# Two single expert slots replaced by one shared slot of 96 and 32 rows in column groups

## The chip, the core and the metric

The kernel runs on one core of a Trainium2 chip. The metric is the device time of one execution in microseconds; before the change it is 801.86, the median of three runs (801.76 to 804.71).

## What is computed

Three stages follow each other on a tensor of 4 batches x 576 tokens x 512 channels: attention with a threshold on the scores, a mixture of experts, and a mixing stage over tokens and channels. The change is in the second:

```python
for b in range(B):
    prev_e = -1
    for s in range(S):
        fresh_e = int(np.argmax(logits[b, s]))
        e = fresh_e if s == 0 or local_gate[b, s] < 0.5 or prev_e < 0 else prev_e
        prev_e = e
        p = np.exp(logits[b, s] - logits[b, s].max()); p /= p.sum() + 1e-09
        h = np.maximum(x[b, s] @ w1[e], 0.0)        # 512 -> 1024
        out[b, s] = p[e] * (h @ w2[e])              # 1024 -> 512
```

There are 8 experts. Each has 2 MB of w1 and 2 MB of w2 in float32. How many tokens each gets depends on the data, so the kernel counts them and reads which expert a piece of work belongs to from a table that it has filled itself.

## The kernel before, in words

**Slots.** Tokens are listed by expert in DRAM. An expert's list is cut into tiles of 128 rows. A *slot* is a piece of work with a fixed place in the program; its expert and its first row come from the table. A paired slot does two tiles of one expert (256 tokens), a single slot does one. Three early slots run while the last batch is still being routed (a single, a pair, a single). Then come eight paired late slots, and then two single ones (`NFINAL = 2`). What doesn't fit runs in extra single slots behind a branch (`self.total > 0`). Which experts get the two single slots is decided in `late_slots` (L691 to L744) by a key: experts with an odd number of tiles left come first, and the two largest keys win. `slot_table` (L746) turns the counts into rows and expert numbers.

**A paired or single slot.** TensorE multiplies in fp32r, with each operand split in a high and a low part, and three products: high x high, high x low, low x high (L1241 to L1243, L1256 to L1258 for pairs; L1272 to L1274, L1317 to L1319 for singles). ScalarE makes the high part and VectorE the low one (L1352, L1355), of w1 into the two tiles `stk`, of w2 into a ring of three. In a single slot the last quarter of w1 and of w2 isn't split; it is multiplied in full fp32 (L1280, L1321). A single slot has tokens as rows of the result, so its hidden values are turned by transposes (L1300) before the second product.

**Order.** TensorE, ScalarE and VectorE run in the order in which the code is written (`manual_schedule`); waits between engines are added by the framework. SP issues all weight loads in its own order: a load waits there until the buffer that it overwrites has been read. The steps of a slot are software-pipelined: `slot_step` handles the slot in hand (`now`), loads and splits the next (`nxt`) and finishes the last (`last`, `old`). A load of w1 or w2 is conditional (`cond`): it is skipped where the expert is that of the slot before.

**Work put in between.** The weights of the third stage come as 64-bit floats and are decoded by VectorE, ScalarE and GpSimd in small steps (`decode`, L1476), some of which stand between a slot's instructions. `more_words` (L1399) has SP stage two pieces of the channel weights, into a ring of two. `load_first_x` (L1619) loads the first batch for the third stage into `raw`, whose space w1 uses till then.

**Behind the last slot.** ScalarE scales the output by the gate (L1335), GpSimd scatters the rows to DRAM (L1342), all engines pass the branch for extra slots (L814), and TensorE begins the third stage with transposes (L1635).

Of the kernel before, what the change touches and what calls it, by code (L numbers as in the profile page):

```python
# [21 lines left out]
DM = H * D  # L22
E, F = 8, 1024
G = E + 1
P = 128
# [6 lines left out]
NEARLY, NTWOS, NFINAL, MAXSINGLE = 2, 8, 2, 8  # L32
# [4 lines left out]
RING, HIDDEN_STEPS, LAST_STEPS = 3, 8, 10  # L37
# [16 lines left out]
class Kernel:  # L54
# [10 lines left out]
    def constants(self):  # L65
# [23 lines left out]
        nc.vector.memset(self.first[0:1, 0:1], -1e30)  # L89
        n = MAXSINGLE  # L90
# [4 lines left out]
        for k, w in ((0, 1), (1, 2), (2, 1), (3, P), (4, 2 * P), (5, P)):  # L95
            nc.gpsimd.iota(i[:, k], pattern=[[w, n]], base=0, channel_multiplier=0)
        self.slotk = self.small("slotk", [1, 2, 3 * n])
        nc.gpsimd.tensor_copy(self.slotk, i[:, :6].rearrange("p (t k) n -> p t (k n)", t=2))
        self.starts = self.small("starts", [1, 3, E + 1])
        nc.gpsimd.memset(self.starts, 1.0)  # L100
        nc.gpsimd.memset(self.starts[:, :, 0:1], 0.0)
        self.late_counts, self.early_counts = (self.small(f"{n}_counts", [1, k, E + 1]) for n, k in (("late", 3), ("early", 2)))
        for t in (self.late_counts, self.early_counts):
            nc.gpsimd.memset(t, 0.0)
        b = scr[0:1, 160:160 + 3 * (E + 1)].rearrange("p (k e) -> p k e", k=3)
        nc.gpsimd.iota(b, pattern=[[0, 3], [NT // P, E + 1]], base=0, channel_multiplier=0)
        self.bases = self.small("bases", [1, 3, E + 1])
# [583 lines left out]
    def late_slots(self):  # L691
# [23 lines left out]
        one, two, fin = (counts[:, k, 1:] for k in range(3))  # L715
        nc.vector.scalar_tensor_tensor(fin, key, top[:, NFINAL - 1:NFINAL], has, ALU.is_ge, ALU.mult)
# [5 lines left out]
        nc.vector.tensor_tensor(bases[:, 2, :E], bases[:, 1, :E], nf, ALU.add)  # L722
# [19 lines left out]
        nc.vector.tensor_tensor(tabi[:, 2, n + 1:], e[:, n + 1:], e[:, n:3 * n - 1], ALU.not_equal)  # L742
# [41 lines left out]
    def first_loads(self):  # L784

        self.w1raw = [self.w1r] + [self.raw[:, i * F:(i + 1) * F] for i in range(3)]
        slots = [("early", 0, False), ("early", NEARLY, True), ("early", 1, False)]
        slots += [("late", MAXSINGLE + j, True) for j in range(NTWOS)]
        slots += [("late", 2 * MAXSINGLE + j, False) for j in range(NFINAL)]
        self.states = [  # L790
            dict(slot=s[:2], two=s[2], first=i == 0, final=i >= len(slots) - NFINAL, extra=False) for i, s in enumerate(slots)]
        self.states[2]["own"] = True
        self.load_index(self.states[0])
        self.load_w1(self.states[0], 0)
        for st in self.states[1:NEARLY + 1]:
            self.load_index(st)

    def experts(self):
        nc, tc = self.nc, self.tc
        self.m_dram = self.scratch["m"]  # L800
        with ExitStack() as ctx:
# [12 lines left out]
            with tc.If(self.total > 0):  # L814
                with ExitStack() as nest:
                    for j in range(MAXSINGLE):
                        if j:
                            nest.enter_context(tc.If(self.total > j))
                        self.run_slots(
                            [dict(slot=("late", j), two=False, first=False, final=False, extra=True)], False)  # L820

                self.load_first_x()
# [25 lines left out]
    def run_slots(self, state, first=True):  # L848
# [26 lines left out]
        for i in range(OPEN_AT + 1 if first else -1, n + 2):  # L875
            if first and i == CHANNEL_AT:
                self.open_channel_weights()
            if first and i >= CHANNEL_AT:
                break
            with self.tc.manual_schedule(engines=MANUAL):  # L880
                self.slot_step(state, i, first)
        if first:
            with self.tc.manual_schedule(engines=MANUAL):
                self.total = self.nc.values_load(
                    self.late["total"][0:1, 0:1], min_val=0, max_val=MAXSINGLE,
                    skip_runtime_bounds_check_because="slots left over by eight experts",
                )
                for i in range(CHANNEL_AT, n + 2):
                    self.slot_step(state, i, first)

    def slot_step(self, state, i, first=True):
# [12 lines left out]
        if now and now["two"]:  # L904
            self.two_step(now, nxt, last if not last["two"] else None, old if old and not old["two"] else None, at(i + 2))
        else:
            self.single_step(
                now, nxt, last if last and not last["two"] else None, old if old and not old["two"] else None,
                first and i == len(state) - 1, first and i == len(state), at(i + 2))

    def two_step(self, now, nxt, last, old, after):
        if after:
            self.load_index(after)
        for c in range(4):
            self.load_w1(nxt, c)
# [18 lines left out]
        for c in range(2):  # L934
            self.split_w1(nxt, c)
# [3 lines left out]
        for c in range(2, 4):  # L939
            self.split_w1(nxt, c)  # L940
        self.decode(STEPS[1] << self.halves)
        spare = None
        if nxt["final"]:
            self.gather(after)
            spare = after["xt"][:, 1]
        for h in range(2):
            self.scale(now, h, spare)
            self.scatter(now, h)

# [107 lines left out]
    def single_step(self, now, nxt, last, old, final, over, after):  # L1057
        ahead = now and nxt and now["final"]
        if now:
            self.hidden_sum(now)  # L1060
            if not ahead:
                self.hidden_last(now)
        if final:
            self.decode(HIDDEN_STEPS)
            self.more_words()
# [4 lines left out]
        if ahead:  # L1070
            nxt["side"] = True
            self.tokens(nxt)
            self.hidden_last(now)
        if now:
            self.relu(now, 0)
        if nxt:
            self.load_w1(nxt, 2)
            self.more_words()
        if now:
            self.relu(now, 1)  # L1080
        if nxt:
            if not ahead:
                self.tokens(nxt)
# [3 lines left out]
        if after and "idx" not in after:  # L1087
            self.load_index(after)
# [7 lines left out]
        if nxt:  # L1096
            for c in range(3):
                self.load_w2(nxt, c)
        if over:
            self.decode(LAST_STEPS)  # L1100
        if old:
            self.scatter(old)
        if final:
            self.load_first_x()
# [5 lines left out]
    def load_index(self, st):  # L1110
# [8 lines left out]
        nc.sync.dma_start(idx, self.list[ds(row, w * P), :].rearrange("(h p) t -> p h t", p=P))  # L1119
# [22 lines left out]
    def tokens(self, st):  # L1142

        nc = self.nc
        if st.get("own"):
# [3 lines left out]
        if not st["two"]:  # L1149
            st["xf"] = xf = self.raw[:, 3 * F + DM:] if st.get("side") else self.xg.tile([P, P], F32, name="xf")  # L1150
# [12 lines left out]
    def load_w1(self, st, i):  # L1163
# [15 lines left out]
        r = self.w1raw[i]  # L1179
# [11 lines left out]
    def load_w2(self, st, i):  # L1191
        if ("w2r", i) not in st:
            st["w2r", i] = True
            self.nc.sync.dma_start(
                self.w2raw[i], self.ins["moe_w2"][ds(st["e"], 1), 2 * i * P:2 * (i + 1) * P, :].rearrange(
# [141 lines left out]
    def scatter(self, st, h=0):  # L1337
# [10 lines left out]
        if st["final"]:  # L1348
# [428 lines left out]
    def run(self):  # L1777
        tc = self.tc
        self.cpool = self.ctx.enter_context(tc.tile_pool(name="const", bufs=1))
        with ExitStack() as self.right:  # L1780
# [7 lines left out]
            with tc.tile_pool(name="area", bufs=1) as area:  # L1788

                self.w1r = area.tile([P, F], F32, name="w1r")  # L1790
                self.stk = [area.tile([P, 4 * F], F32R, name=f"stk{i}") for i in range(2)]
# [58 lines left out]
```

## Time and profile before

| | |
|---|---|
| median of three runs | 801.86 us (801.76 to 804.71) |
| profiled execution | 802.82 us, span 801.1 us |
| TensorE busy | 766.5 us (96%) |
| VectorE busy | 597.6 us (75%) |
| ScalarE busy | 487.2 us (61%) |
| DMA | 111.18 MB, mean 139 GB/s |
| mean granted clock | 0.995 |

The span is the time from the first to the last instruction; the rest of an execution lies around it. Busy is the union of an engine's instructions: TensorE's matmuls overlap each other in the profile, since one begins while the one before still drains, so the time from one start to the next is what counts there. Attention takes the span to some 290 us, the experts to some 558 us, mixing the rest.

### The profile page before, as it was taken

The numbers are of one execution on the slowest core, as the hardware profiler recorded it, in microseconds if no ns is written. First come the engines' busy times: TensorE is split into PE (matmuls) and PEld (weight loads), VectorE is DVE, ScalarE is ACT, GpSimd is POOL, SyncE is SP. The second block draws the span as 40 slices with busy tenths as digits, with TensorE's granted clock in tenths as the row PEclk, the third lists the DMA queues.
The fourth block names the chain that finished last, engine by engine and source line by source line (L and its number), as shares of the span: only waits on it lengthen the run. The fifth ranks groups of instructions, "written<-read, shape, count | busy, mean of one in ns | idle before, by whom it ended". The sixth has DMA issues, their size and how long they took to land.

```text
span 801.1 us, 16558 instructions
## 1 busy us (share of the span) xinstructions
PE 766.5 (96%) x6234; PEld 624.8 (78%) x6234; DVE 597.6 (75%) x1258; ACT 487.2 (61%) x963; POOL 199.9 (25%) x238
## 2 busy tenths in 40 slices
PE   7899999999999989999999999998899999999997
PEld 4455565565555478789999899975899999999996
DVE  6999899998989688659788889677795446555522
ACT  5998888887867664555555566464855345434411
POOL 4000003002102113335455465434002122033110
PEclk9999999999999999999999999999999999999999
DMA  6622323332411578798877787675010110110101
GB/s 158 182 75 75 98 76 89 109 95 63 134 50 60 192 287 228 255 353 294 286 224 261 263 289 242 231 264 185 16 53 1 61 66 1 54 59 2 60 1 60
DMA packets 69472, 111.18 MB, mean 139 GB/s; under 512 B 28546, under 2 KB 35078, under 8 KB 69384
## 3 DMA queue, kind: packets, MB, share of 16 engines
q1 hardware_dynamic: 65192, 99.52, 39.0%
q0 software_dynamic: 4192, 10.51, 3.7%
q8 instruction: 52, 0.85, 0.5%
q14 instruction: 36, 0.29, 0.1%
HBM read 94.48 MB, written 16.58 MB: 139 GB/s over the span
## 4 chain that ended last, share of the span: by engine, by line
PE 64%; DVE 13%; DMA 10%; issue 5%; ACT 4%; POOL 2%; SPq 1%; DVEq 0%; ACTq 0%; POOLq 0%
PE o L431 6%; PE s L307 6%; PE y L1729 5%; PE y L1728 5%; PE y L1727 5%; DMA scr_m<-xt,idx 4%; PE t L400 4%; DVE a L366 3%; DMA raw<-in_moe_w_dram 3%; DVE ns L326 2%; PE v L1758 2%; PE v L1759 2%; PE v L1757 2%; PE o L1257 2%; PE o L1258 2%
## 5 line engine op out<-in xcount | busy, mean ns | idle before, releaser
L326 DVE TENSOR_SCALAR_CACHE_REDUCE ns<-s,nqs 128x576 f32<-128x576 f32 x144 | 116.7, 811 | 19.1 <-PE s L307 16.8
L366 DVE SCALAR_TENSOR_TENSOR a<-ns,thr,e 128x576 f32<-128x576 f32 x144 | 116.9, 812 | 0.6 <-ACT thr L339 0.6
L332 ACT ACTIVATE e<-ns,nb 128x576 f32<-128x576 f32 x144 | 109.7, 782 | 9.9 <-DVE ns L326 9.9
L407 ACT ACTIVATE aT<-t 128x256 f32<-128x256 f32 (+1 forms) x216 | 82.6, 458 | 33.1 <-PE t L400 32.3
L307 PE MATMUL s<-raw 64*128 64x288 f32 x512 | 82.7, 435 | 8.9 <-ACT aT L393 4.9
L431 PE MATMUL o<-aT,vm 128*64 128x288 f32 x512 | 76.2, 421 | 0.0
L1241 PE MATMUL h<-xh,stk 128*128 128x256 f32 x256 | 72.9, 285 | 0.0
L1242 PE MATMUL h<-xl,stk 128*128 128x256 f32 x256 | 72.4, 283 | 0.0
L1243 PE MATMUL h<-xh,stk 128*128 128x256 f32 x256 | 72.4, 283 | 0.0
L1355 DVE TENSOR_TENSOR w2l<-w2r,w2h 128x1024 fp32r<-128x1024 f32 x48 | 61.2, 1284 | 10.1 <-ACT w2h L1352 9.8
L307 PEld LDWEIGHTS s<-raw 64*128 64x128 f32 x512 | 44.2, 193 | 23.1 <-DVE ns L326 8.3
L431 PEld LDWEIGHTS o<-aT,vm 128*64 128x64 f32 x512 | 33.2, 138 | 33.4 <-issue 14.5
L1256 PE MATMUL o<-w2h,hh 128*128 128x512 f32 x144 | 57.0, 396 | 0.0
L1257 PE MATMUL o<-w2l,hh 128*128 128x512 f32 x144 | 56.4, 392 | 0.2 <-DVE w2l L1355 0.2
L1352 ACT ACTIVATE w2h<-w2r 128x1024 fp32r<-128x1024 f32 x48 | 50.1, 1054 | 10.5 <-issue 7.9
L1258 PE MATMUL o<-w2h,hl 128*128 128x512 f32 x144 | 56.2, 390 | 0.0
L400 PEld LDWEIGHTS t<-ident,a 64*128 64x128 f32 x1152 | 42.4, 139 | 16.0 <-ACT e L332 6.7
L400 PE MATMUL t<-ident,a 64*128 64x64 f32 x1152 | 51.5, 228 | 0.3 <-ACT aT L407 0.2
L1229 ACT ACTIVATE hh<-h 128x512 fp32r<-128x512 f32 x36 | 21.3, 598 | 48.0 <-PE h L1243 42.6
L1241 PEld LDWEIGHTS h<-xh,stk 128*128 128x128 f32 x256 | 49.1, 192 | 1.3 <-DVE hl L1230 1.0
L1242 PEld LDWEIGHTS h<-xl,stk 128*128 128x128 f32 x256 | 49.1, 192 | 0.5 <-issue 0.2
L1243 PEld LDWEIGHTS h<-xh,stk 128*128 128x128 f32 x256 | 49.1, 192 | 0.0
(366 smaller groups left out, 2084.8 us busy)
## 6 DMA issues: line engine op xcount, KB each, us to landing
w2r<-in_moe_w_dram SPq DMA_DIRECT2D x52, 512.0 KB, 5.5
raw<-in_moe_w_dram SPq DMA_DIRECT2D x39, 512.0 KB, 8.0
raw<-in_q_dram SPq DMA_DIRECT2D x15, 576.0 KB, 4.8
w1r<-in_moe_w_dram SPq DMA_DIRECT2D x13, 512.0 KB, 4.2
raw<-in_k_dram SPq DMA_DIRECT2D x30, 176.0 KB, 4.3
vm<-in_v_dram SPq DMA_DIRECT2D x32, 128.0 KB, 2.6
out_dram<-ob SPq DMA_DIRECT2D x16, 256.0 KB, 2.2
scr_x<-x SPq DMA_DIRECT2D x12, 256.0 KB, 4.2
```

Of the source, the lines that this page charges most:

```text
L307: nc.tensor.matmul(s[:, z, :SH], qd[rows, int(j != z), cs], kd[rows, j * KH:j * KH + SH], start=True, stop=True)
L326: nc.vector.tensor_scalar(ns, s[:, :, :SH], self.nqs[:, 0:1], None, ALU.mult, ALU.min, accum_out=nb)
L332: self.nc.scalar.activation(e, pr["s", c, j], AF.Exp, bias=pr["nb", c][:, j:j + 1], scale=-1.0)
L366: nc.vector.scalar_tensor_tensor(a.rearrange("p (z s) -> p z s", z=2), s, thr, e, ALU.is_le, ALU.mult, accum_out=total)
L400: nc.tensor.transpose(t[h][:, 4 * n + b], a[r, (k + b) * P:(k + b + 1) * P], self.ident[r, r])
L407: nc.scalar.activation(self.pairs[i]["aT"][:, b:b + w, s0:s0 + D], t[h][:, 4 * n:4 * n + w], AF.Copy)
L431: self.last_av = nc.tensor.matmul(o[j * D:(j + 1) * D, :SH], vm[:, j, c - 1, :], aT[:, 4 * j + c - 1, zs], start=(z == 0 and c == 1), stop ...
L1241: nc.tensor.matmul(h[:, i], wh[:, fs], xh, start=(k == 0), stop=False)
L1242: nc.tensor.matmul(h[:, i], wh[:, fs], xl, start=False, stop=False)
L1243: nc.tensor.matmul(h[:, i], wl[:, fs], xh, start=False, stop=(k == 3))
L1257: nc.tensor.matmul(o, hh, wl[:, i], start=False, stop=False)
L1258: nc.tensor.matmul(o, hl, wh[:, i], start=False, stop=(q == 3 and i == 1))
```

## The change

The two single late slots become one slot with two parts: up to 96 rows of one expert (`big`) and up to 32 rows of another (`few`). Each matmul is issued three times into the same bank of the accumulator: columns 0 to 63 and 64 to 95 of the array with the first expert's weights, columns 96 to 127 with the second's. Nothing is split: all of the slot is in full fp32, from the raw weights. The first expert's lie where a single slot's lay; the second's are loaded into the space of `stk`, which is reopened as fp32. `late_slots` now also looks at the rows of each expert's last tile: `big` goes to an expert with 33 to 96 rows there, `few` to one with at most 32, again odd numbers of tiles first. The table grows from three kinds of slot to four.

```diff
-NEARLY, NTWOS, NFINAL, MAXSINGLE = 2, 8, 2, 8
+NEARLY, NTWOS, MAXSINGLE = 2, 8, 8
+SHARE = 96, 32
...
-RING, HIDDEN_STEPS, LAST_STEPS = 3, 8, 10
+RING, SHARED_STEPS = 3, (4, 4, 10)
...
+        rows = self.small("late_rows", [1, E], I32)
+        nc.vector.tensor_scalar(rows, ni, P - 1, None, ALU.bitwise_and)
         nc.vector.tensor_scalar(ni, ni, 7, None, ALU.logical_shift_right)
...
+        nc.vector.tensor_tensor(
+            self.late_keys[:, :, :E], rows.unsqueeze(1).to_broadcast([1, 2, E]),
+            self.share.unsqueeze(2).to_broadcast([1, 2, E]), ALU.is_lt)
...
-        top = self.small("late_top", [1, 8])
-        nc.vector.max(top, key)
...
-        nc.vector.scalar_tensor_tensor(fin, key, top[:, NFINAL - 1:NFINAL], has, ALU.is_ge, ALU.mult)
+        nc.vector.tensor_tensor(last, last, key.unsqueeze(1).to_broadcast([1, 2, E]), ALU.mult)
+        nc.vector.tensor_tensor(last[:, 0], last[:, 0], last[:, 1], ALU.subtract)
+        tops = self.small("late_tops", [1, 2])
+        nc.vector.tensor_reduce(tops, keys, AX.X, ALU.max)
+        nc.vector.tensor_tensor(
+            counts[:, 2:, 1:], last, tops.unsqueeze(2).to_broadcast([1, 2, E]), ALU.is_ge)
+        fin = self.small("late_fin", [1, E])
+        nc.vector.tensor_tensor(fin, big, few, ALU.add)
...
+        if few:
+            views = [[t[:, i * F:(i + 1) * F] for i in range(4)] for t in self.open_stk(F32)]
+            few["w1raw"] = views[0]
+            few["w2raw"] = [v.rearrange("p (t f) -> p t f", t=2) for v in views[1]]
+            for c in range(4):
+                self.load_w1(few, c)
+        else:
+            for c in range(2):
+                self.split_w1(nxt, c)
         self.split_w2(now, 3)
         self.load_w2(nxt, 3)
         self.finish_two(now, 3)
-        for c in range(2, 4):
-            self.split_w1(nxt, c)
+        if few:
+            for c in range(4):
+                self.load_w2(few, c)
...
+    def shared_slot(self, st):
+        nc = self.nc
+        few, cols = st["few"], []
+        for a, b, w in ((0, 64, st), (64, SHARE[0], st), (SHARE[0], P, few)):
+            cols.append((slice(a, b), w.get("w1raw", self.w1raw), w.get("w2raw", self.w2raw)))
+        self.more_words()
+        h = self.hg.tile([P, F], F32, name="h")
+        hf = self.xg.tile([P, 4, 2 * P], F32, name="xl").rearrange("p a b -> p (a b)")
+
+        def turn(z):
+            t = self.ps_x.tile([P, 4, P], F32, name="t").rearrange("p a b -> p (a b)")
+            for i in range(4):
+                nc.tensor.transpose(
+                    t[:, i * P:(i + 1) * P], h[:, z * 512 + i * P:z * 512 + (i + 1) * P], self.ident)
+            nc.scalar.activation(hf[:, z * 512:(z + 1) * 512], t, AF.Copy)
+        for z in range(2):
+            zs = slice(z * 512, (z + 1) * 512)
+            hp = self.ps_h.tile([P, 2, 2 * P], F32, name="h").rearrange("p a b -> p (a b)")
+            for k in range(4):
+                for c, w1, _ in cols:
+                    nc.tensor.matmul(
+                        hp[c], st["xf"][:, k, c], w1[k][:, zs], start=(k == 0), stop=(k == 3), skip_group_check=True)
+                if z and k == 1:
+                    turn(0)
+            nc.scalar.activation(h[:, zs], hp, AF.Relu)
+            self.decode(SHARED_STEPS[z])
+        self.load_first_x()
+        self.more_words()
+        st["o"] = o = self.ps_o.tile([P, DM], F32, name="o")
+        for k in range(8):
+            for c, _, w2 in cols:
+                nc.tensor.matmul(
+                    o[c], hf[:, k * P:(k + 1) * P][:, c], w2[k // 2][:, k % 2], start=(k == 0), stop=(k == 7),
+                    skip_group_check=True)
+            if k == 1:
+                turn(1)
+        self.decode(SHARED_STEPS[2])
+        self.scale(st)
+        self.scatter(st)
```

TensorE, from the last product of the eighth pair on, before (`xh` and `xl` are the split tokens, `xf` and `raw` the unsplit quarter):

```order
L1258 MATMUL o<-w2h,hl 128x512
L1272 MATMUL h<-stk_78,xh 128x512
L1273 MATMUL h<-stk_78,xh 128x512
L1274 MATMUL h<-stk_78,xl 128x512
...
L1154 MATMUL t<-ident,xt 128x128 x4
L1280 MATMUL h<-raw,xf 128x512 x2
L1300 MATMUL t<-ident,h 128x128 x8
```

The same place after (`stk_7139` holds the second expert's raw w1; the tokens lie in `xh` now):

```order
L1321 MATMUL o<-w2h,hl 128x512
L997 MATMUL h<-w1r,xh 64x512
L997 MATMUL h<-w1r,xh 32x512
L997 MATMUL h<-stk_7139,xh 32x512
L997 MATMUL h<-raw,xh 64x512
L997 MATMUL h<-raw,xh 32x512
L997 MATMUL h<-stk_7139,xh 32x512
```

The split products of two slots, 36 each and 4 in fp32, are gone; in their place stand 16 groups of one matmul of 64 and two of 32 columns, with two sets of four transposes between them.

VectorE, in the choice of the slots, before:

```order
L711 TENSOR_TENSOR late_key<-late_key,late_has 1x8
L713 MAX late_top<-late_key 1x8
L716 SCALAR_TENSOR_TENSOR late_counts<-late_key,late_top,late_has 1x8
L719 TENSOR_TENSOR late_ni<-late_nf,late_counts 1x8
L720 TENSOR_TENSOR late_nf<-late_nf,late_counts 1x8
```

and after:

```order
L722 TENSOR_TENSOR late_key<-late_key,late_has 1x8
L727 TENSOR_TENSOR late_keys<-late_keys,late_key 1x2x8
L728 TENSOR_TENSOR late_keys<-late_keys 1x8
L730 TENSOR_REDUCE late_tops<-late_keys 1x2
L731 TENSOR_TENSOR late_counts<-late_keys,late_tops 1x2x8
L734 TENSOR_TENSOR late_fin<-late_counts 1x8
L737 TENSOR_TENSOR late_ni<-late_nf,late_fin 1x8
```

Two operations became five here; further up two more come in (the rows and the masks), further down one (a fourth base).

SP's loads behind the last pair's, after (`w` are channel words, `raw<-scr_m` the first batch for the third stage):

```order
L1486 DMA w_7087<-in_moe_w_ch_dram 128x512
L1486 DMA w_7089<-in_moe_w_ch_dram 128x512
L1236 TENSOR_LOAD late_tabi
...
L1243 DMA stk_7139<-in_moe_w_dram 128x1024
...
L1257 DMA w2r_4464<-in_moe_w_dram 128x2x512
...
L1257 DMA stk_7140<-in_moe_w_dram 128x2x512
...
L1486 DMA w_7193<-in_moe_w_ch_dram 128x512
L1486 DMA w_7195<-in_moe_w_ch_dram 128x512
L1687 DMA raw<-scr_m 128x512 x4
L1687 DMA raw<-scr_m 64x512
L1486 DMA w_7254<-in_moe_w_ch_dram 128x512
L1486 DMA w_7256<-in_moe_w_ch_dram 128x512
```

The second expert's four loads of w1 and four of w2 now stand ahead of the third pair of channel words, and the last pair of words stands behind the loads of the first batch; before, those loads were spread among the weight loads of the second single slot.

## Rows read from the trace of the kernel before

**Rows 1.** The page, part 1: busy time and share of the span, instructions.
```profile
PE 766.5 (96%) x6234; PEld 624.8 (78%) x6234; DVE 597.6 (75%) x1258; ACT 487.2 (61%) x963; POOL 199.9 (25%) x238
```

**Rows 2.** Timeline of TensorE, the two single slots: start, duration, instruction, count, [idle, releaser].
```profile
529.82 0.39 PE L1272 MATMUL h<-stk,xh 128*128 128x512 f32 x1
...
534.34 1.88 PE L1280 MATMUL h<-raw,xf 128*128 128x512 f32 x4
536.06 0.65 PE L1300 MATMUL t<-ident,h 128*128 128x128 f32 x4
...
542.66 1.98 PE L1280 MATMUL h<-raw 128*128 128x512 f32 x4 [0.98 <-DMA raw<-in_moe_w_dram]
...
550.30 1.04 PE L1300 MATMUL t<-ident,h 128*128 128x128 f32 x8
...
556.22 1.88 PE L1321 MATMUL o<-w2r,hf 128*128 128x512 f32 x4
558.92 0.33 PE L1635 MATMUL v<-ident,raw 128*128 128x128 f32 x1 [0.83 <-ACT raw L1335]
```

**Rows 3.** Stage table, that stretch: length, busy PE, PEld, DVE, ACT, POOL, granted clock, DMA share, GB/s.
```profile
529.80:558.90 29.10, 26.72 (x109) 18.18 (x107) 21.04 (x33) 18.24 (x30) 10.96 (x13) 1.00 0.64 218
```

**Rows 4.** Timeline of TensorE in attention: rows*columns of the array, moving operand, passes.
```profile
154.33 1.19 PE L431 MATMUL o<-aT,vm 128*64 128x288 f32 x8
155.45 0.69 PE L464 MATMUL g<-xT,wg 128*32 128x288 f32 x8
156.07 0.34 PE L400 MATMUL t<-ident,a 64*128 64x64 f32 x4
```

**Rows 5.** Timeline of VectorE, the choice of the late slots.
```profile
304.67 0.14 DVE L697 TENSOR_TENSOR late_ni<-left,g 1x8 int32<-1x8 f32 x1
...
305.71 0.16 DVE L711 TENSOR_TENSOR late_key<-late_key,late_has 1x8 f32<-1x8 f32 x1
305.90 0.16 DVE L713 MAX8 late_top<-late_key 1x8 f32<-1x8 f32 x1
...
306.34 0.16 DVE L719 TENSOR_TENSOR late_ni<-late_nf,late_counts 1x8 int32<-1x8 f32 x1
...
307.85 0.15 DVE L731 TENSOR_TENSOR bases<-bases,late_counts 1x8 f32<-1x8 f32 x1
```

**Rows 6.** Timeline of TensorE, its weight loads and GpSimd, beside and behind that choice.
```profile
308.04 1.88 PE L1321 MATMUL o<-w2r,hf 128*128 128x512 f32 x4
309.79 0.19 PEld L1241 LDWEIGHTS h<-xh,stk 128*128 128x128 f32 x1 [0.70 <-DVE hl L1230]
...
321.42 1.95 POOL L1137 DMA_INDIRECT xt<-scr_x,idx  x1 [0.30 <-issue]
...
331.09 1.03 PE L1154 MATMUL t<-ident,xt 128*128 128x128 f32 x8
```

**Rows 7.** The page, part 5: splits of a w2 part; busy, mean ns | idle before, releaser.
```profile
L1355 DVE TENSOR_TENSOR w2l<-w2r,w2h 128x1024 fp32r<-128x1024 f32 x48 | 61.2, 1284 | 10.1 <-ACT w2h L1352 9.8
```

**Rows 8.** Timeline of SP's issues, last pair and single slots.
```profile
518.62 0.37 SPq L1194 DMA_DIRECT2D w2r<-in_moe_w_dram  x1
519.11 0.88 SPq L1423 DMA_DIRECT2D w<-in_moe_w_ch_dram  x2
...
545.17 0.83 SPq L1423 DMA_DIRECT2D w<-in_moe_w_ch_dram  x2
```

**Rows 9.** Stage table, the end of the last pair.
```profile
520.00:530.00 10.00, 10.00 (x45) 8.28 (x45) 8.48 (x14) 5.03 (x7) 3.68 (x6) 1.00 0.87 290
```

**Rows 10.** Timeline of GpSimd: first use of the last channel word.
```profile
550.79 0.98 POOL L1458 TENSOR_TENSOR ch<-w 128x256 fp32r<-128x256 f32 x1 [0.57 <-DMA w<-in_moe_w_ch_dram]
```

**Rows 11.** Timeline of VectorE: start of the last words' decoding.
```profile
552.65 2.11 DVE L1457 TENSOR_SCALAR val<-w 128x256 int32<-128x256 int32 x2
```

**Rows 12.** Timeline of ScalarE: end of the last words' decoding, and the last scale.
```profile
556.52 0.75 ACT L1449 ACTIVATE ch<-val 128x256 fp32r<-128x256 f32 x2 [3.69 <-DVE val L1466]
558.18 0.69 ACT L1335 ACTIVATE raw<-o,idx 128x512 f32<-128x512 f32 x1 [0.91 <-PEq L814]
```

More of the change, by code (lines that the diff above doesn't have):

```diff
@@ L711, in late_slots @@
         nc.vector.tensor_tensor(key, key, has, ALU.mult)
-        top = self.small("late_top", [1, 8])
-        nc.vector.max(top, key)
         counts, bases = self.late_counts, self.bases
-        one, two, fin = (counts[:, k, 1:] for k in range(3))
-        nc.vector.scalar_tensor_tensor(fin, key, top[:, NFINAL - 1:NFINAL], has, ALU.is_ge, ALU.mult)
+        one, two, big, few = (counts[:, k, 1:] for k in range(4))
+        keys = self.late_keys
+        last = keys[:, :, :E]
+        nc.vector.tensor_tensor(last, last, key.unsqueeze(1).to_broadcast([1, 2, E]), ALU.mult)
[6 more added lines that the diff above has]
+        nc.vector.tensor_tensor(fin, big, few, ALU.add)
         yield
@@ L788, in first_loads @@
         slots += [("late", MAXSINGLE + j, True) for j in range(NTWOS)]
-        slots += [("late", 2 * MAXSINGLE + j, False) for j in range(NFINAL)]
-        self.states = [
-            dict(slot=s[:2], two=s[2], first=i == 0, final=i >= len(slots) - NFINAL, extra=False) for i, s in enumerate(slots)]
+        slots += [("late", 2 * MAXSINGLE, False)]
+        self.states = [dict(slot=s[:2], two=s[2], first=i == 0, extra=False) for i, s in enumerate(slots)]
+        self.states[-1]["few"] = dict(slot=("late", 3 * MAXSINGLE), first=True)
         self.states[2]["own"] = True
@@ L819, in experts @@
                         self.run_slots(
-                            [dict(slot=("late", j), two=False, first=False, final=False, extra=True)], False)
+                            [dict(slot=("late", j), two=False, first=False, extra=True)], False)
                 self.load_first_x()
@@ L904, in slot_step, with two_step @@
         if now and now["two"]:
-            self.two_step(now, nxt, last if not last["two"] else None, old if old and not old["two"] else None, at(i + 2))
+            self.two_step(now, nxt, last if not last["two"] else None, at(i + 2))
         else:
             self.single_step(
-                now, nxt, last if last and not last["two"] else None, old if old and not old["two"] else None,
-                first and i == len(state) - 1, first and i == len(state), at(i + 2))
-    def two_step(self, now, nxt, last, old, after):
+                now, nxt, last if last and not last["two"] else None, old if old and not old["two"] else None)
+    def two_step(self, now, nxt, last, after):
         if after:
             self.load_index(after)
+        few = nxt.get("few")
         for c in range(4):
@@ L938, in two_step @@
         self.finish_two(now, 3)
-        for c in range(2, 4):
-            self.split_w1(nxt, c)
+        if few:
+            for c in range(4):
+                self.load_w2(few, c)
+        else:
+            for c in range(2, 4):
+                self.split_w1(nxt, c)
         self.decode(STEPS[1] << self.halves)
[L942 to L945, printed above, removed]
         for h in range(2):
-            self.scale(now, h, spare)
+            self.scale(now, h, nxt["xt"][:, 1] if few else None)
@@ L1055, in store_last, with single_step @@
             next(self.last_x, None)
-    def single_step(self, now, nxt, last, old, final, over, after):
-        ahead = now and nxt and now["final"]
+    def single_step(self, now, nxt, last, old):
         if now:
             self.hidden_sum(now)
[L1061 to L1065, printed above, removed]
+            self.hidden_last(now)
         if nxt:
@@ L1081, in single_step @@
         if nxt:
-            if not ahead:
-                self.tokens(nxt)
+            self.tokens(nxt)
             self.load_w1(nxt, 3)
@@ L1149, in tokens @@
         if not st["two"]:
-            st["xf"] = xf = self.raw[:, 3 * F + DM:] if st.get("side") else self.xg.tile([P, P], F32, name="xf")
+            st["xf"] = xf = self.xg.tile([P, P], F32, name="xf")
         for h in range(1 + st["two"]):
```

77 lines of the change are left out of this document (43 added, 34 removed).

## The prediction

> **What bounds the kernel now.** I read the page's first part, then TensorE's timeline of the stretch that the change rewrites, then the stage table of that stretch, and last every wait that is inside it. TensorE is busy 96% of the span [rows 1], so whatever leaves or enters its queue shows in the time unless another engine is late. The reader is to see in its timeline that the first of the two single slots begins at 529.82 [rows 2]. From there the two slots run to the last fp32 matmul, L1321. Four of its passes take 1.72 us: L1280's four begin at 534.34 and the next instruction at 536.06, 0.43 each (an fp32 matmul is two records here). So the work ends at 556.22 + 1.72 = 557.94, and the stretch is **28.1 us**. It holds small idle times (the longest 0.98, on a weight load of the second slot [rows 2]). Granted clock in it is 1.00, the 2.4 GHz level [rows 3]. After it comes a fixed tail: ScalarE's scale, the branch, the first transposes of mixing at 558.92.
>
> **Who gets the new slot.** I counted tokens per expert with the reference's own inputs. Expert 7 has 82 tokens in its last tile, expert 0 has 9; the old rule gives the two single slots to expert 0 and then 7, the new one gives the 96 rows to 7 and the 32 rows to 0. The other tiles make eight full pairs in both, so no extra slot runs in either. The last paired slot is expert 7's, so the conditional loads of the wide part find its weights in place; only expert 0's 4 MB are loaded, into the space of the split weights.
>
> **TensorE's new stretch.** The two slots leave with all their work, 28.1 us. What comes is 16 groups (8 for the hidden layer, 8 for the output), each one matmul of 64 columns of the array and two of 32, all over 512 moving columns in fp32, two passes each. If the three ran side by side, a group would be 0.86; if the 64 ran first and then the two 32s together, 1.72; one by one, 2.58. The trace has no group of mixed width, so this is the term to bound. What it does have is equal widths side by side, and a change of width between such stretches [rows 4]. L431 (64 columns, two abreast) does 8 passes of 288 columns, four steps of 0.43 x 288/512 = 0.24, together 0.97; it begins at 154.33 and the next stretch at 155.45, so it takes 1.12. L464 (32 columns, four abreast) does 8 passes in two steps, 0.48, and takes 0.62 to 156.07. So equal widths do run abreast at full rate, and each stretch of one width costs some 0.15 and 0.14 more than its streams. I take that excess to be an emptying of the array when the width changes, because both borders show it. That says what happens between two stretches that want the same columns; whether 64 at one place and 32 beside it also wait for each other no row tells. I take the rows' nearest case, that every change of width waits.
>
> The Trainium skill, page "TensorEngine Tiling (Array Packing)", section "Key Properties", has a rule against the change: a new tiling mode, as opposed to another tile of the same one, drains TensorE. The excess of 0.14 to 0.15 agrees with it where it can be seen; by it the three matmuls of a group cannot overlap and the sum is the one that follows.
>
> A group is then 0.86 + 0.15 + 0.86 + 0.14 = 2.01, and 16 are 32.2. Two sets of four transposes of the hidden values stand between them: eight take 1.04 and four 0.65 [rows 2], so four stream 0.39, with a change of width 0.54 each, 1.1 together. New stretch **33.2 us**, against 28.1: **+5.1**. Bounds of this term: 16 x 0.86 + 1.1 + 0.2 = 15.1 (-13.0) and 48 x (0.86 + 0.14) + 1.1 = 49.1 (+21.0).
>
> **The routing chain.** VectorE chooses the slots between 304.67 and 308.0, in small dependent operations about 0.19 apart [rows 5]. Behind them in its queue stand a weight split (L1355) and the hl of the first pair (L1230). PE's weight load at 309.79 waits for that hl [rows 6], while its work before ends at 308.04 + 1.72 = 309.76: slack 0.03. The change takes out L713 and L716 (from 305.90 to 306.34, 0.44) and adds eight: five in the chain (the keys times the masks, their difference, the maxima, the comparison, the sum), 5 x 0.19 = 0.95, and three beside it (the row counts, the masks, one more base), 0.08 to 0.19 each. Net 0.75 to 1.1; **+0.9**, and it reaches TensorE, because the later waits of this phase hang on TensorE's own ends. The table behind it grows by a third (four kinds of slot for three), which I put at 0.4. What follows from the table is the next slot's gather, issued by 323.4 for tokens that TensorE turns at 331.09 [rows 6]: some 7 us less the transfer, so 1.3 us more cost nothing.
>
> **What goes beside other work.** The 12 splits of both slots on ScalarE and VectorE (1.28 for a w2 part on the latter [rows 7]) disappear; neither engine was ahead of TensorE for longer than the idle times already counted in the 28.1. For the narrow expert's w1, SP reaches its loads behind the two word loads of 519.11 [rows 8]: 4 x 0.52 MB and 0.52 MB of words at 290 GB/s [rows 9] are 9 us, 528; the first is wanted at 529.8, the last three groups later. Its w2 follow by 535 and are wanted after 8 groups. Cost 0 while that holds; if it fails, the lateness of the first load, up to 2 us. SP still issues the skipped loads with their waits: no row shows one. Between 0 and what an issue takes (0.37 [rows 8]), eight are at most 3 us of SP, which no one waits for then. 0.
>
> **Sum.** 5.1 + 0.9 = **+6.0**. The profiled execution was 802.82 (span 801.10 and 1.72 around it), so 808.8 by its clock; the median of the runs shown is 0.96 lower, and I predict from that: 801.86 + 6.0 = **807.9**. Its own range: with half the excess per change 805.5, with 0.20 per change and 1.2 for the routing 810.
>
> **Rival 1, the other side: all three abreast.** The columns of a group's matmuls don't overlap, and rows 4 show four tiles with four different moving operands at full rate; if the array only waits where columns overlap, the stretch is 15.1 us and TensorE is done at 529.8 + 15.1 = 544.9. The Trainium skill, page "TensorE: Matmul & The Clock Gate", Part 3, describes tiles by a mask of 32-column strips and a span of one matmul for several tiles, which speaks for this rival. Then something else is late: the last two channel words. They are staged behind the loads of x, which wait for the hidden matmuls (537.4), so SP issues them near 538.5. Now they are issued at 545.17 and the second is used at 550.79 [rows 8, 10], 5.6 later; from VectorE's start on them at 552.65 to ScalarE's end at 556.52 + 0.75 it takes 4.6 [rows 11, 12]. So 538.5 + 5.6 + 4.6 = 548.7, and the scale stands behind them in ScalarE's queue, as it did at 558.18 [rows 12]. Gain 9.5, less the 0.9: 801.86 - 8.6 = **793.3**, between 790 (words in time) and 797 (words or weights later). This decides from the point where a group takes less than 1.7 us. Against it: the excess at each change of width.
>
> **Rival 2: one by one.** The 32s don't overlap either: +21.0 + 0.9, **823.8**. L464 speaks against it.
>
> **Rival 3: the change doesn't do what it says.** If the narrow part found no expert, an odd tile would run in an extra slot, some 14 us (half of 28.1) with its loads uncovered: about 820. The counts exclude it for these inputs.
>
> **How the numbers follow.** Forecast 0.61, rival 1 0.34, rival 2 0.04, rival 3 0.01. What a measurement of this kernel can tell from no change is about 0.5%, 4.0 us: faster is below 797.9, slower above 805.9. Rival 1 lies below but for 0.01; of the forecast's 0.61, 0.07 lies within. Faster 0.33, same 0.08, slower 0.59. Forecast and rival 1 lie on both sides of the present time and neither can be left out for 8 in 10: the range is 791 to 810; the forecast's own is 805.5 to 810.
>
> **What would show it.** In the profile after: the starts of the 32-column matmuls of a group some 1.0 us behind the 64-column one (forecast), within 0.02 us (rival 1), or the two 32s apart (rival 2); TensorE's stretch from the first of them to the last near 33 us; PE's weight load for L1241's successor some 0.9 us later than 309.79 with VectorE as its releaser; no wait for the narrow expert's loads. The forecast is wrong if a group takes clearly less than 1.7 us, and its size is wrong if a change of width costs less among disjoint columns than between stretches.

## The result and the profile after

The changed kernel takes **810.07 us** (median of six runs, 809.36 to 810.97). The kernel before took 803.87 in six runs (801.76 to 805.07), 2.0 more than in the three runs that the prediction had. The ratio is 1.0082, with a 95% interval of 1.0062 to 1.0101: slower by 6.6 us (5.0 to 8.1); the two medians differ by 6.2. The profiled execution has a span of 807.6, 6.5 more than before.

TensorE's timeline at the start of the shared slot (start, us, engine, line, operation, tiles, rows*columns of the array, moving operand, passes) answers to [rows 2]:

```profile
529.21 1.62 PE L997 MATMUL h<-w1r,xh 128*64 128x512 f32 x3
530.22 0.62 PE L997 MATMUL h<-stk,xh 128*32 128x512 f32 x1
530.67 0.59 PE L997 MATMUL h<-w1r,xh 128*32 128x512 f32 x1
530.67 0.59 PE L997 MATMUL h<-stk,xh 128*32 128x512 f32 x1
531.20 1.62 PE L997 MATMUL h<-raw,xh 128*64 128x512 f32 x3
532.21 0.62 PE L997 MATMUL h<-stk,xh 128*32 128x512 f32 x1
...
561.62 0.59 PE L1008 MATMUL o<-stk,xl 128*32 128x512 f32 x1
563.08 1.97 PE L1698 MATMUL v<-ident,raw 128*128 128x128 f32 x16 [0.86 <-ACTq L833]
```

A row of three passes holds the two 64-column passes and the first 32-column pass of the wide expert, which read the same tiles. The reader is to see that the narrow expert's pass (tile `stk`) begins 1.01 behind the 64-column ones, at 530.22, and that the two 32s then run together. The next group begins at 531.20, so a group is 1.99. No row of the stretch waits for a load. The slot ends at 561.62 + 0.43 = 562.05: **32.84 us** from 529.21, against 28.12 [rows 2]. Its row in the stage table answers to [rows 3] (length, busy PE, PEld, DVE, ACT, POOL, granted clock, DMA share, GB/s):

```profile
529.20:562.10 32.90, 32.90 (x105) 6.20 (x104) 7.89 (x16) 5.05 (x11) 8.66 (x12) 1.00 0.37 127
```

TensorE is busy throughout and its weight loads are not: the time is matmuls that follow one another.

At the end of the routing chain, TensorE's work and its weight load answer to [rows 6]:

```profile
306.07 1.88 PE L1384 MATMUL o<-w2r,hf 128*128 128x512 f32 x4
308.55 0.19 PEld L1304 LDWEIGHTS h<-xh,stk 128*128 128x128 f32 x1 [1.43 <-DVE hl L1293]
```

The work ahead ends at 306.07 + 1.72 = 307.79 and the weight load begins at 308.55, so the wait is 0.76 where it was 0.03: **+0.73**. (The work ahead ends 1.97 earlier than before, from attention, which the change doesn't touch; the mean granted clock from 100 to 290 is 1.00 here and 0.98 before. In the twelve profiles of this case the first row stands anywhere from 306.07 to 317.52.) From the end of that work to the slot's first pass it takes 221.42, against 220.06 before: 0.73 of the 1.36 is this wait. The other 0.63 lies in the eight pairs, where TensorE waits 0.9 for VectorE's splits of w2, against 0.2 before. In nine profiles of kernels that are alike in this stretch it takes anywhere from 220.0 to 221.9.

Behind the slot, TensorE's timeline and stage table go on:

```profile
570.99 0.84 PE L1698 MATMUL v<-ident,raw 128*128 128x128 f32 x4 [2.92 <-DMA raw<-scr_m]
571.48 0.56 PE L1719 MATMUL th<-th,xTh 128*128 128x256 f32 x1
...
584.35 0.29 PE L1790 MATMUL y<-wt,zrh 128*128 128x288 f32 x1
...
801.35 1.47 PE L1832 MATMUL v<-ident,u 128*64 128x128 f32 x12
```

```profile
568.00:570.00 2.00, 0.07 (x1) 0.00 (x0) 0.06 (x1) 0.67 (x2) 0.00 (x0) 1.00 0.11 41
570.00:572.00 2.00, 1.01 (x6) 1.04 (x7) 0.00 (x0) 0.13 (x1) 0.00 (x0) 0.81 0.07 25
572.00:574.00 2.00, 2.00 (x12) 2.00 (x11) 1.07 (x2) 1.59 (x4) 0.46 (x1) 0.50 0.00 0
```

The fifth token tile of the mixing stage (the transposes at 570.99) holds rows that the last slot has only just scattered. TensorE idles 2.92 for it, and then the granted clock is 0.50, the 1.2 GHz level, while VectorE and ScalarE aren't waited for. The kernel before has the same two places and the same last row:

```profile
566.56 0.63 PE L1635 MATMUL v<-ident,raw 128*128 128x128 f32 x4 [1.05 <-DMA raw<-scr_m]
...
578.33 0.29 PE L1727 MATMUL y<-wt,zrh 128*128 128x288 f32 x1
...
794.36 1.47 PE L1769 MATMUL v<-ident,u 128*64 128x128 f32 x12
```

From the slot's end to the first mix matmul (`y`) it took 578.33 - 557.94 = 20.39 and now takes 584.35 - 562.05 = 22.30: +1.9. From there to the last group of transposes it took 216.03 and now takes 217.00: +0.97, without one wait that stands out. Neither was in the prediction's sum. The half clock has 1.5 of the +1.9: from the transposes at 570.99 to the sixteenth matmul behind them it takes 3.78, and 2.23 before.

### The profile page after: what moved, and what is told of

Same layout as the page of the kernel before. It is cut to its first block, busy times and chain, and to the rows that moved or that the text cites. A ratio compares the mean times of both kernels' runs of the same rounds, so it can differ in the third digit from the quotient of the medians.

```text
span 807.6 us, 16486 instructions
## 1 busy us (share of the span) xinstructions
PE 773.2 (96%) x6230; PEld 614.3 (76%) x6230; DVE 582.1 (72%) x1246; ACT 471.9 (58%) x941; POOL 196.0 (24%) x241
## 5 line engine op out<-in xcount | busy, mean ns | idle before, releaser
L1418 DVE TENSOR_TENSOR w2l<-w2r,w2h 128x1024 fp32r<-128x1024 f32 x42 | 54.6, 1306 | 11.6 <-ACT w2h L1415 11.6
L1415 ACT ACTIVATE w2h<-w2r 128x1024 fp32r<-128x1024 f32 x42 | 44.0, 1054 | 10.9 <-issue 7.9
```

## The experiments

Each kernel is compared by its ratio to the kernel before, which ran beside it on the same chip. There that took 803.03 beside the first four, and on another chip 806.6 beside the next four and 807.1 beside the last two.

**Four matmuls of one width per group.**

```
-for a, b, w in ((0, 64, st), (64, SHARE[0], st), (SHARE[0], P, few)):
+for a, b, w in ((0, 32, st), (32, 64, st), (64, SHARE[0], st), (SHARE[0], P, few)):
```

> The changed kernel with its 64-column matmul cut into two of 32, so that a group is four matmuls of one width (three with the wide expert's weights, one with the narrow one's); same arithmetic. Theory (a change of width makes the array wait, equal widths run abreast): a group takes 0.86 to 0.95 in place of 1.985, the 16 groups with their two sets of transposes about 15 to 16.5 us in place of 32.8, TensorE is done near 545; then the last channel words are late and the scale starts near 549 in place of 562, so the time falls by 9 to 13 us against the changed kernel, to 797 to 801. Rival (matmuls with different weights and different moving data do not run side by side in this stretch, whatever their width): four matmuls in at least two steps, a group 1.9 or more, time 808 to 812, or 24 us longer if they run one by one.

Measured: 796.33, ratio 0.9933 (0.9908 to 0.9957): faster than both kernels, and 5.4 us (3.5 to 7.4) under the kernel before. Its timeline of TensorE:

```profile
530.67 0.63 PE L997 MATMUL h<-w1r,xh 128*32 128x512 f32 x3
530.69 0.62 PE L997 MATMUL h<-stk,xh 128*32 128x512 f32 x1
531.12 0.61 PE L997 MATMUL h<-w1r,xh 128*32 128x512 f32 x3
...
531.55 0.61 PE L997 MATMUL h<-raw,xh 128*32 128x512 f32 x3
...
532.41 0.61 PE L997 MATMUL h<-raw,xh 128*32 128x512 f32 x3
...
545.46 0.59 PE L1008 MATMUL o<-stk,xl 128*32 128x512 f32 x1
549.79 1.97 PE L1698 MATMUL v<-ident,raw 128*128 128x128 f32 x16 [3.74 <-ACTq L833]
558.23 1.09 PE L1698 MATMUL v<-ident,raw 128*128 128x128 f32 x4 [3.45 <-DMA raw<-scr_m]
```

The narrow expert's pass begins 0.02 behind the first of the three others (one row of three), and the next four 0.43 to 0.45 later, so a group is 0.86 (531.55 to 532.41) and the stretch 15.2 (530.67 to 545.46 + 0.43). Matmuls with different tokens in the array and two different moving operands (the weights of the two experts) do run abreast, and the rival falls. Then ScalarE is late, as rival 1 of the prediction had it (548.7):

```profile
548.41 0.75 ACT L1512 ACTIVATE ch<-val 128x256 fp32r<-128x256 f32 x2 [6.37 <-DVE val L1529]
549.07 0.67 ACT L1398 ACTIVATE raw<-o,idx 128x512 f32<-128x512 f32 x1
```

The scale stands behind the last channel words and starts 3.2 after TensorE is done.

**The same matmuls, ordered by width** (hidden layer shown; the output likewise).

```
-for k in range(4):
-    for c, w1, _ in cols:
+for k in range(8):
+    k, part = k % 4, cols[:1] if k < 4 else cols[1:]
+    for c, w1, _ in part:
```

> The changed kernel with the matmuls of a half ordered by width: the four 64-column ones first, then the four pairs of 32 columns; same matmuls, 10 stretches of one width in place of 34. Theory (a border between widths costs 0.14 to 0.15 and nothing overlaps across it): the stretch falls from 32.8 by 24 x 0.145 = 3.5 to about 29.3, time about 806.5. Rival 1 (widths overlap in part inside a group, so 1.985 already holds an overlap): no gain or a loss, 810 or more. Rival 2 (the excess belongs to each matmul's weight load, not to the border): no change in the stretch, 810.

Measured: 807.14, ratio 1.0046 (1.0033 to 1.0059). TensorE's timeline, the first stretch of 64 columns and the start of the first of 32, then the end:

```profile
532.51 1.07 PE L998 MATMUL h<-w1r,xh 128*64 128x512 f32 x2
533.42 2.74 PE L998 MATMUL h<-raw,xh 128*64 128x512 f32 x6
536.09 0.62 PE L998 MATMUL h<-stk,xh 128*32 128x512 f32 x1
...
561.70 0.59 PE L1011 MATMUL o<-stk,xl 128*32 128x512 f32 x1
...
570.85 0.63 PE L1701 MATMUL v<-ident,raw 128*128 128x128 f32 x4 [2.71 <-DMA raw<-scr_m]
...
582.67 0.30 PE L1793 MATMUL y<-wt,zrh 128*128 128x288 f32 x1
```

Eight 64-column passes take 3.58 (532.51 to 536.09), 0.14 more than 8 x 0.43. From the first pass to the last start it is 29.19, against 32.41, and 24 borders fewer: **0.134 a border**. The price is the border's, not the matmul's. The ratio's interval lies below the changed kernel's (1.0062 to 1.0101). Behind the slot, the idle time of 2.71 was not followed by a lower clock here, and from 562.13 to the first mix matmul it took 20.54, as before the change (20.39). So most of the changed kernel's +1.9 behind the slot is the clock in that one execution.

**Mixing's matmuls into that idle time.**

```
 self.theta(0, 0, 0)
+self.theta(0, 0, 1)
 self.prep(0, (4,), (2,))
 for dh in range(2):
-    for g in range(1 - dh, 3):
+    for g in range(2 - 2 * dh, 3):
```

> The changed kernel with one block of mixing's matmuls (the theta of the third and fourth tile, 24 matmuls, 2.8 us) moved ahead of the transposes of the fifth tile, which wait for the last scattered rows. Theory (behind the slot the chain scale, scatter, load back ends last; TensorE idles 2.92 before those transposes and then runs 3.5 us at a granted clock of 0.5): the idle time shrinks to 0 to 0.3, the granted clock stays at 1.00, the first mix matmul is 3.5 to 4.3 us earlier, time 806 to 807. Rival (the wave work on ScalarE and VectorE behind it is as late as TensorE, so it becomes the wait): gain under 1.5 us, a wait on VectorE or ScalarE at the first mix matmul, time 809 to 810.

Measured: 808.88, ratio 1.0074 (1.0055 to 1.0093), not to be told from the changed kernel's. The idle time is gone and the clock stays at 1.00; the first mix matmul comes 19.30 after the slot's end (563.72 to 583.02), 3.0 sooner. But from there it takes 218.52 to the last transposes, 1.5 more, and the new wait is VectorE's:

```profile
584.18 0.40 PE L1793 MATMUL y<-wt,zrl 128*128 128x288 f32 x1 [0.73 <-DVE zrl L1780]
586.26 0.40 PE L1793 MATMUL y<-wt,zrl 128*128 128x288 f32 x1 [0.22 <-DVE zrl L1780]
```

These two account for 0.95 of the 1.5. The rival holds in its mechanism: half of what the filler gives is lost again, and the 806 to 807 of the theory wasn't reached. Beside executions in which the clock doesn't fall (20.54 above, 20.83 with padding below) the filler gives only 1.2 to 1.5, and the 1.5 use that up.

**The routing chain alone, in the kernel before.**

```
 nc.vector.tensor_tensor(key, key, has, ALU.mult)
+for _ in range(16):
+    nc.vector.tensor_tensor(key, key, has, ALU.mult)
```

> The kernel before with 16 more dependent VectorE operations (key times mask, repeated) in the chain that chooses the late slots; same result. Theory (that chain ends in the weight load of the first pair with a slack of 0.03): the weight load is 16 x 0.19 = 3.0 us later, and all behind it, time 801.9 to 803.9 + 3.0. Rival (the lateness is caught up at a later wait of this phase, which hangs on loads or on VectorE and ScalarE): the weight load is 3.0 later but TensorE's first single slot less than 1 us.

Measured: 808.35, ratio 1.0063 (1.0047 to 1.0080). Its timeline:

```profile
306.30 1.88 PE L1323 MATMUL o<-w2r,hf 128*128 128x512 f32 x4
311.07 0.19 PEld L1243 LDWEIGHTS h<-xh,stk 128*128 128x128 f32 x1 [3.72 <-DVE hl L1232]
```

Work ends at 308.02 and the load begins at 311.07: 3.05, against 0.03, so 16 operations cost 3.02, 0.19 each. From 308.02 to the first single slot (531.47) it takes 223.45, against 220.06 before: the delay is still there, and the rival falls. At the weight load the chain reaches TensorE one to one; at the slot that is so within the 1.9 by which this stretch varies. The timed 5.1 us (3.8 to 6.4) is more than the 3.0 that the trace accounts for, and the profiled execution, the fastest of the six, has a span of only 802.2. The mean granted clock goes with it: 0.996 and 0.997 in the two shortest executions (805.72 and 803.92), 0.988 to 0.994 in the other four (808.02 to 809.28). What lowered the clock in these stays open.

**Scale and scatter first**, on top of four matmuls.

```
-self.decode(SHARED_STEPS[2])
 self.scale(st)
 self.scatter(st)
+self.decode(SHARED_STEPS[2])
```

> The kernel with four 32-column matmuls per group, and in addition the shared slot's scale and scatter stand ahead of the decoding of the last channel words on ScalarE (there the scale waited from TensorE's end near 545.9 to 549.07). Theory (behind the slot the chain scale, scatter, load back, fifth tile's transposes ends last): the scale starts near 546.5, the fifth tile's transposes near 554.8 in place of 558.23, TensorE's idle time before them falls from 3.4 to under 1, the granted clock does not fall, time about 791 to 793. Rival (the last words' decoding itself holds the branch and all of mixing, so the end of the slot does not matter): the first transposes of mixing stay at 549.8 and the time within 1 us of the kernel with four matmuls, 796.

Measured: 799.03, ratio 0.9893 (0.9871 to 0.9915); the interval of four matmuls alone (0.9908 to 0.9957) overlaps it at the edge. From the slot's end (550.65) to the first mix matmul (573.16) it is 22.51, against 25.65 (545.89 to 571.54) with four matmuls alone. ScalarE's timeline shows both theories at work, and TensorE's row below it what stands in the way:

```profile
550.95 0.69 ACT L1398 ACTIVATE raw<-o,idx 128x512 f32<-128x512 f32 x1 [4.80 <-PE o L1008]
551.54 0.71 ACT L1512 ACTIVATE ch<-val 128x256 fp32r<-128x256 f32 x2
556.50 0.42 ACT L1512 ACTIVATE ch<-val 128x256 fp32r<-128x256 f32 x1 [4.25 <-DVEq L833]
556.99 0.60 ACT L1699 ACTIVATE xTh<-v 128x512 fp32r<-128x512 f32 x1
```

```profile
553.77 3.59 PE L1698 MATMUL v<-ident,raw 128*128 128x128 f32 x16 [2.96 <-PEq L833]
```

The scale follows the last matmul at once, but the split of words that were ready earlier (551.54) slipped behind it too, and with it the decoding of the last ones, behind which mixing's first copies (556.99) wait. The branch still holds TensorE for 2.96, and the clock falls behind it (mean 0.53 from 553.7 to 556.0), which the theory had ruled out. The fifth tile is no longer waited for.

**Mixing's filler and wave work first**, on top of that: `theta(0, 0, 1)` and `wave("01" "000")` ahead of `prep(0, (4,), (2,))`.

> The kernel with the scale first, and in addition mixing's block of 24 theta matmuls and the first steps of its wave work moved ahead of the fifth tile's transposes. Theory (with the scale first the fifth tile is no longer late by more than 0.3, so there is nothing left to fill): within 1 us of the kernel with the scale first, 790 to 793. Rival (the fifth tile is still the wait, or VectorE's wave work is the next bound and starts earlier here): 2 to 4 us less than that kernel.

Measured: 799.51, ratio 0.9912 (0.9882 to 0.9942). No gain, as the theory had it; the intervals of the two overlap. That nothing was left to fill isn't shown: behind the slot TensorE has other idle times here (1.86, 2.88 and 0.83), and from the slot's end (546.90) to the last transposes it takes 241.8, against 239.7 with the scale first.

**Where the operands lie**: the changed kernel with 32 bytes of padding behind its table, the kernel before with 96.

```
+self.nc.gpsimd.memset(self.cpool.tile([1, 8], F32, name="pad"), 0.0)    # [1, 24] in the kernel before
 self.late["total"] = total = self.cpool.tile([1, 1], I32, name="late_total")
```

> The changed kernel with 32 bytes of padding behind its slot table, so that all buffers allocated behind it stand 128 bytes further on than in the kernel before, in place of 96. Theory (mixing's matmuls run 0.5% slower in the changed kernel because the table grew by 96 bytes and its operands lie at another offset): from the first mix matmul to the last TensorE instruction 217.2 to 217.5 us, as in the kernel before, in place of 218.2. Rival (another cause, or chance): 218.0 or more.

> The kernel before with 96 bytes of padding at the place where the changed kernel's slot table is longer, and nothing else. Theory (offset of the operands): from the first mix matmul to the last TensorE instruction 218.0 to 218.4 us in place of 217.2. Rival: 217.2 to 217.5.

The idle time before the fifth tile and the first and last row of mixing, the changed kernel with padding, and then first and last row of the kernel before with padding:

```profile
582.65 0.63 PE L1699 MATMUL v<-ident,raw 128*128 128x128 f32 x4 [3.13 <-DMA raw<-scr_m]
...
594.42 0.30 PE L1791 MATMUL y<-wt,zrh 128*128 128x288 f32 x1
...
810.51 1.47 PE L1833 MATMUL v<-ident,u 128*64 128x128 f32 x12
```

```profile
584.37 0.29 PE L1728 MATMUL y<-wt,zrh 128*128 128x288 f32 x1
...
801.57 1.47 PE L1770 MATMUL v<-ident,u 128*64 128x128 f32 x12
```

216.09 and 217.20 between these rows. (To the start of the very last matmul, the measure of the expectation, 217.29 and 218.41.) Shifted by 0 or 128 bytes, mixing takes 216.0 to 216.5 (the kernel before, the longer chain, this one, and the kernel with everything together below); shifted by 96, 217.0 to 217.2 (the changed kernel, four matmuls, ordered by width, scale first, two matmuls of 64, this one). The two kernels with mixing's work in another order are left out of this. The +0.97 is the table's 96 bytes. Each of the two was run once, and the claim rests on the traces, not on their times of 818.53 and 810.06. What the 818.53 has too much lies ahead of the late slots: the work before the routing chain ends at 319.24, against 307.79 in the changed kernel, and the mean granted clock from 290 to 317 is 0.86. Behind the slot, the changed kernel with padding takes 20.83 to the first mix matmul: 3.13 of idle time, and no fall of the clock.

**Everything together**: four matmuls, ready words split before the scale, last words decoded after it, 32 bytes of padding.

```
+for _ in range(2):
+    self.split_last(self.last)
 self.scale(st)
 self.scatter(st)
 self.decode(SHARED_STEPS[2])
```

> Everything that the runs so far point to, together: four 32-column matmuls per group; the words decoded already are split, then the slot is scaled and scattered, and only then the last words are decoded; 32 bytes of padding behind the slot table. Theory (three terms that add): 13 us from the widths less the late words, some 5 us of the chain behind the slot (first mix matmul 20.9 us after the last matmul of the slot starts, against 26.1 with four matmuls alone and 22.9 with the scale simply first), 1.0 us from the offsets in mixing; the time is 1.2 to 1.6% below the kernel before, about 791 where that takes 803. Rival (the decoding of the last words bounds mixing whatever stands before it): no better than the kernel with the scale first, 1.1% below the kernel before.

Measured: 797.82, **ratio 0.9874 (0.9849 to 0.9899)**, 1.3% under the kernel before and the lowest that was run. Its interval lies below that of four matmuls alone, but overlaps that of the scale first. Its tail, in TensorE's timeline and in the stage table:

```profile
548.35 0.59 PE L1009 MATMUL o<-stk,xl 128*32 128x512 f32 x1
551.80 3.48 PE L1701 MATMUL v<-ident,raw 128*128 128x128 f32 x16 [2.87 <-SPq L834]
558.93 0.63 PE L1701 MATMUL v<-ident,raw 128*128 128x128 f32 x4 [0.82 <-DMA raw<-scr_m]
```

```profile
551.80:556.00 4.20, 4.20 (x24) 4.20 (x25) 2.35 (x6) 2.07 (x5) 1.61 (x3) 0.62 0.16 54
```

The first mix matmul (570.30) comes 21.95 after 548.35, a microsecond more than expected: the branch still holds TensorE for 2.87, and the clock fell behind that (mean 0.62 from 551.8 to 556.0). Mixing takes 216.50, 0.5 less than with four matmuls alone, where 1.0 was expected.

**Two matmuls of 64 columns.**

```
-for a, b, w in ((0, 64, st), (64, SHARE[0], st), (SHARE[0], P, few)):
+for a, b, w in ((0, 64, st), (64, P, few)):
```

> The changed kernel with two matmuls of 64 columns per group, one per expert; the wide expert's rows 64 to 95 are left out (they are computed with the narrow expert's weights). Theory (one width per group, so nothing waits, whatever the width): a group takes 0.86, the shared slot 15 to 15.5 us, as with four of 32. Rival (only the narrowest tiles run abreast with different moving data): a group takes 1.7 or more.

TensorE's timeline in its one run (801.14; the kernel leaves out rows, so its time isn't compared):

```profile
534.26 0.64 PE L997 MATMUL h<-w1r,xh 128*64 128x512 f32 x1
534.27 0.64 PE L997 MATMUL h<-stk,xh 128*64 128x512 f32 x1
...
535.17 0.59 PE L997 MATMUL h<-raw,xh 128*64 128x512 f32 x1
...
536.03 0.59 PE L997 MATMUL h<-raw,xh 128*64 128x512 f32 x1
```

The two begin 0.01 apart and the next group 0.91 later; later groups are 0.86 (535.17 to 536.03), and the whole slot takes 15.3. It is the equal width that counts, not the width of 32.

## Why the prediction was wrong, step by step

It forecast the right side, mechanism and size, and its range ended just below the result: 810.07 against an upper end of 810.0.

| step of the prediction | forecast | in the runs |
|---|---|---|
| one group | 2.01 | 1.99 |
| the slot's stretch | 33.2, +5.1 | 32.84, +4.7 |
| a change of width | 0.14 to 0.15 | 0.134 |
| routing chain | +0.9 | +0.73 |
| the eight pairs, up to the slot | 0 | +0.63 |
| slot's end to first mix matmul | "fixed tail", 0 | +1.9 in this profile, 1.5 of it the clock; +0.15 and +0.4 in two others, where it doesn't fall |
| mixing from there on | 0 | +0.97 |
| attention; behind the last transposes | 0 | -1.97; -0.44 |
| sum | +6.0 | +6.5 between the two profiles; timed +6.6 (5.0 to 8.1) |

**The widths** were the term to be bounded, and the nearest rows were the right ones: the excess at a border in attention [rows 4] is the excess here. The Trainium skill, page "TensorEngine Tiling (Array Packing)", section "Key Properties", says that a new tiling mode drains the engine where another tile of the same mode does not; the changed kernel and three experiments agree with it (1.99 a group of mixed width, 0.86 of one width, 0.134 a border). The prediction still gave 0.34 to the rival that disjoint columns don't wait. The time of its scale came out once the widths were equal (548.7, measured 549.07), in part by luck: SP issued the last words 10.8 behind the slot's first pass, where 8.7 was forecast, and from there they were used and decoded faster (4.5 and 4.05, for 5.6 and 4.6). Behind the scale the rival had nothing more to lose, but the first mix matmul came 22.47 after it, against 20.15 before, so the gain was 5.4 and not 8.6. And its condition doesn't hold for mixed widths.

**The routing chain** came out at 0.73 for 0.9: from its first operation (L697, now L703) to the weight split behind it, VectorE takes 4.00 where it took 3.26. 0.61 of that lies where five operations stand for two, the rest in those beside them. The chain made longer on its own shows that such operations reach TensorE's weight load in full.

**Loads and the skipped issues** were put at 0, and no row of the slot waits for one.

**The step that failed is the sum's last one: the base it was put on, and two terms it put at nothing.** First the base: 6.0 was put on the median of three runs, 801.86, though the profiled execution was 0.96 above it; six runs have it at 803.87. With that base the forecast is 809.9, so 2.0 of the miss of 2.2 is the base, and the range had no room for it, though three runs of one kernel had already spread over 3.0 us. Second, "after it comes a fixed tail": mixing's code was unchanged, but its buffers moved by 96 bytes with the table, which costs 0.97, and the idle time ahead of the fifth tile grew from 1.05 to 2.92, behind which the clock may fall (1.5 in the profile shown). These were offset in part by a stretch 0.4 and a chain 0.2 shorter than forecast. That the +6.0 came within 0.6 of the timed +6.6 is therefore in part luck: terms left out, and executions that differ by some us in attention, nearly cancel.

What stays open: how often the clock falls there. It did behind idle times of 2.92, 3.45 (four matmuls), 2.96 (scale first) and 2.87 (everything together). It didn't behind 2.71 (ordered by width), 3.13 (padding) and 3.74 (four matmuls, ahead of mixing's first transposes, 549.79). So the length of the idle time alone doesn't decide it.

## What to carry to other kernels

Pack column tiles of one width into a group: cutting a 64-column matmul in two of 32, which adds instructions, took a group from 1.99 to 0.86 us, since matmuls of one width overlap, and every change of width costs 0.13 us and ends the overlap. When a stretch gets shorter, look at once for what stands behind it in the queues of the other engines (here the last words ahead of the scale, 3.2 us). Put a forecast of under 1% on a base with its own spread, and look at what a grown table shifts.

## What the runs showed of the hardware

- Moving by 96 bytes all buffers behind the slot table made the stretch of mixing's matmuls 0.4 to 0.5% longer (217.0 to 217.2 us against 216.0 to 216.5); 32 bytes more undid it. Which operand it is, weights or moving data, was not taken apart.
- Two fp32 matmuls of 64 columns, or four of 32, with different stationary and two different moving operands take 0.86 us for two passes of 512 columns each; a full-width one takes 0.43 a pass.
- A group of one 64-column matmul and two of 32 on columns that don't overlap takes 1.99 us: every change of width costs 0.134 us, and nothing overlaps across it.
- After an idle time of about 3 us the granted clock sometimes fell to 0.50 for the next matmuls and sometimes not: the same place in the program cost 22.30 us in one execution of the changed kernel, and 20.83 with 32 bytes of padding.
